# Moving a softmax ratio to GpSimd and reordering two other steps in a fused attention and gated-MLP kernel

## The chip, the cores and the metric

The kernel runs on one core of one Trainium2 chip. A core has five engines that run side by side, each in the order of its own instruction list: TensorE (PE in the profile; its weight loads are PEld), VectorE (DVE), ScalarE (ACT), GpSimd (POOL) and SyncE (SP, which only issues transfers here). They wait for each other through semaphores. The metric is the time of one execution on the device, in microseconds (us), as the median of several runs.

## The reference, cut to what matters

Two token mixers share one input `x` (2048 tokens of 512 values), and a gate per token blends them.

```
g   = sigmoid(sum(x * gate_w))
# mixer A: 32 heads of 16 values
q, k, v = x @ wqkv ;  pq = q @ w_phi ;  pk = k @ w_phi          (per head)
phi(p)  = concat(softmax(p), softmax(-p))                       (32 features per head)
kv  = phi(pk)^T @ v ;  z = sum over tokens of phi(pk)
a   = (phi(pq) @ kv) / (phi(pq) @ z + 1e-6) @ wo
# mixer B
z1, z2 = halves of gelu(x @ w_in) ;  z2 = layernorm(z2)
b   = (z1 * (w_sp @ z2 + b_sp)) @ w_out                          (w_sp: 2048 x 2048)
out = g * a + (1 - g) * b
```

## The kernel before

**Stages.** From 0 to about 44 us it computes `z1` and `z2` (`z_mm`, line 208). From 44 to about 124 us a loop over 16 tiles of 128 tokens makes the features of the keys (`k_tile`), the values (`v_tile`) and their product `kvacc` (`kv_acc`), four of the 16 query tiles (`q_tile`), and, interleaved, steps of the spatial product `w_sp @ z2`. From there to the end the remaining query tiles, the attention tiles (`attn_tile`), the rest of the spatial product and the output projections (`ba_tile`) run.

**The spatial product.** The rows of `w_sp` are taken as eight pairs p of row tiles (p and p+8). Pairs 0 and 5 are multiplied plainly (`plain`). The other six go by a scheme of seven products of half size instead of eight (`product(p, k)`, k = 1 to 7). It needs scaled sums of the weight blocks. For each pair ACT takes magnitudes of both halves (`w_size`, line 342, which the diff calls a magnitude pass: |w| summed per row; it also fills a scratch tile). DVE adds the two row sums (`wsum`, 347), PE sums over the rows (`w_level`, 351), and DVE makes the scale `wdown` and its inverse `wup` (352, 355). ACT scales one half by `wup` (`w_scale`, 370, about 2 us). Then `w_sum` forms the sums: S3 on DVE (358, output `wmix`), S1 on GpSimd (375), S2 on DVE (377), S4 on DVE (358, output `wsp`). A pair takes three steps of the token loop: (5, 2), (6, the next pair's 1, 7), (4, 3).

**Banks.** The products add up in three PSUM banks. One of them is opened by product 5 (`start=True`), read by DVE after product 7 and again after product 3 (`plus`, line 570, output `c`). So product 3 waits for the first read, and the next pair's product 5 for the second. `v_tile` has one bank: the values of tile t+1 can only be written when DVE has read those of tile t (`vr`, line 487). Attention tiles share one bank too, read by DVE at lines 613 and 614 (`o`).

**Features.** `expo` multiplies, takes exp(p) and exp(-p) on ACT (443) and sums each over the 16 features of a head on DVE (`zs`, 447). DVE takes reciprocals (`rk`, 456; `rq`, 473). `even_out` then forms a ratio of the two sums per head (462, 128 x 32 numbers, on DVE) and GpSimd multiplies the second half of the features by it (463). So both halves share one normaliser. For keys that normaliser goes into the values: `vr` is v times `rk`, and GpSimd copies `rk` itself beside it (486). The tile `zs` has two buffers, shared by keys and queries.

**What sets the order.** The lists of PE and ACT are in the order of the program text (`manual_schedule`). Those of DVE, GpSimd and SP come from a scheduler that takes ready instructions by priority. In the token loop, `prepare(tt, w_size)` stands ahead of the value tile, or, in every third tile, behind the first product of the step.

Of the kernel before, what the change touches and what calls it, by code (L numbers as in the profile page):

```python
# [8 lines left out]
ALU = mybir.AluOpType  # L9
# [5 lines left out]
P = 128  # L15
# [3 lines left out]
DH = 16  # L19
# [9 lines left out]
NG = 4  # L29
# [12 lines left out]
def kernel(  # L42
# [14 lines left out]
    nc = tc.nc  # L57
# [58 lines left out]
        out=ramp[:, 0, :], data0=ones32[:, :], data1=zeros[:, :], initial=0.0,  # L116
# [4 lines left out]
    for q in range(4):  # L121
        qs = slice(32 * q, 32 * q + 32)
        nc.vector.tensor_tensor(
            out=ident[qs, qs], in0=ramp[qs, 0, :], in1=ramp[qs, 1, :], op=ALU.is_equal)
    nc.gpsimd.memset(brow[:], 0.0)
    nc.gpsimd.memset(wphi[:], 0.0)
    def load_z2w(eng, dt):
# [11 lines left out]
        out=scrap[:, :], in_=nc.const_aps.tensor(1.0, [P, 1], BF16), func=AF.Gelu_apprx_tanh)  # L139
# [6 lines left out]
    for h in range(2):  # L146
        nc.sync.dma_start(
            out=w_z1[:, 2 * h:2 * h + 2, :], in_=w_in_v[:, 2 * h:2 * h + 2, 0:FH])
    for i in range(4, 8):
        x_dma_T(i)  # L150
    for q in range(2, NCH):
        nc.sync.dma_start_transpose(
            out=xT[:, :, q * CH:(q + 1) * CH], in_=x2[q * CH:(q + 1) * CH, :]
# [3 lines left out]
    for qk in (1, 0):  # L157
        nc.sync.dma_start_transpose(
            out=wqkT[:, qk * NDT:(qk + 1) * NDT, :], in_=A_wqkv[:, qk * D:(qk + 1) * D])
# [13 lines left out]
    for p in range(NRING):  # L173
# [4 lines left out]
        out=mask4[:], in_=mask4[:], pattern=[[-32, NG]],  # L178
# [3 lines left out]
        out=mask4[:], in_=mask4[:], pattern=[[32, NG]],  # L182
# [3 lines left out]
        out=mask64[:, :, :], in_=mask4[:, :, None].to_broadcast([P, NG, DH]))  # L186
# [204 lines left out]
    def z_sum(part, i):  # L391
        c = slice(4 * part, 4 * part + 4)
        out, a, op, b = Z_SUMS[i]
        nc.vector.tensor_tensor(
            out=zsums[out][:, c, :], in0=zsums[a][:, c, :], in1=zsums[b][:, c, :], op=op)
# [35 lines left out]
    def bank_tile(tag):  # L431
        return psM.tile([P, CH], FP32, name="mm", tag=tag)
# [20 lines left out]
    def k_tile(tt, bank):  # L453
        ek, z = expo(kvp, "ek", 5, tt, wk_p, bank_tile(bank))
        rk = kvp.tile([P, H, 2], FP32, name="rk", bufs=3)
        nc.vector.reciprocal(out=rk[:], in_=z[:])  # L456
        even_out(ek, z, rk[:, :, 1])
        return ek, rk

    def even_out(e, z, rz):  # L460
        ratio = work.tile([P, H], FP32, name="ratio")
        nc.vector.tensor_tensor(out=ratio[:], in0=z[:, :, 0], in1=rz, op=ALU.mult)  # L462
        nc.gpsimd.tensor_tensor(  # L463
            out=e[:, :, 1, :], in0=e[:, :, 1, :],
            in1=ratio[:, :, None].to_broadcast([P, H, DH]), op=ALU.mult)
# [4 lines left out]
    def q_tile(n, ps):  # L470
        eq, z = expo(work, "eq", 3, token(n), wq_p, ps)
        rq = work.tile([P, H], FP32, name="rq")
        nc.vector.reciprocal(out=rq[:], in_=z[:, :, 1])
        even_out(eq, z, rq[:])
        eqT = work.tile([P, 8, P], BF16, name="eqT", bufs=7)
        nc.sync.dma_start_transpose(out=eqT[:, :, :], in_=eq[:].rearrange("p h a f -> p (h a f)"))
        eqTs[n] = eqT

    def v_tile(tt, rk, bank):
        v_ps = bank_tile(bank)  # L480
        for dt in range(NDT):
            nc.tensor.matmul(v_ps[:, :], lhsT=xT[:, dt, tt * P:(tt + 1) * P], rhs=wv_sb[:, dt, :],  # L482
                             start=(dt == 0), stop=(dt == NDT - 1))
        vr = kvp.tile([P, 8, AW], BF16, name="vr", bufs=4)
        r0 = rk[:, :, 0].rearrange("p (u h) -> p u h", u=8)
        nc.gpsimd.tensor_copy(out=vr[:, :, 64:AW], in_=r0)
        nc.vector.tensor_tensor(  # L487
            out=vr[:, :, 0:64].rearrange("p u (h d) -> p u h d", d=DH),
            in0=v_ps[:, :].rearrange("p (u h d) -> p u h d", u=8, d=DH),
            in1=r0[:, :, :, None].to_broadcast([P, 8, NG, DH]),  # L490
            op=ALU.mult,
        )
        return vr

    def kv_acc(tt, ek, vr):
        ekf = ek[:].rearrange("p h a f -> p (h a f)")
        for g in range(8):
            nc.tensor.matmul(
                kvacc[:, g, 0:AW], lhsT=ekf[:, g * P:(g + 1) * P], rhs=vr[:, g, :],
                start=(tt == 0 and g % 4 == 0), stop=(tt == NT - 1), skip_group_check=True,  # L500
            )

    def kvz_evac():
        nc.vector.tensor_tensor(
            out=kvz[:, :, 0:64], in0=kvacc[:, :, 0:64],
            in1=mask64[:].rearrange("p h d -> p (h d)")[:, None, :].to_broadcast([P, 8, 64]),
            op=ALU.mult,
        )
        nc.vector.scalar_tensor_tensor(
            out=kvz[:, :, 64:AW], in0=kvacc[:, :, 64:AW],  # L510
            scalar=0.5e-6, in1=mask4[:, None, :].to_broadcast([P, 8, NG]),
            op0=ALU.add, op1=ALU.mult,
        )
# [157 lines left out]
    steps, work_at = [], {}  # L671
# [28 lines left out]
    def prepare(n, *kinds):  # L700
        for f, *args in work_at.get(n, ()):
            if f in kinds:
                f(*args)

    def level(n):
        for f, p, *_ in work_at.get(n, ()):
            if f is w_scale:
                w_level(p, bank_tile(Q_BANK if n < NT else X_TAGS[2]))
# [3 lines left out]
    with tc.manual_schedule(engines={mybir.EngineType.PE, mybir.EngineType.Activation}):  # L712
        ks = {0: k_tile(0, Q_BANK)}
        kvacc = psM.tile([P, 8, P], FP32, name="kvacc", tag="kvat", bufs=1)
        pend = []
        for tt in range(NT):
            if tt + 1 < NT:
                ks[tt + 1] = k_tile(tt + 1, K_BANK)
            prepare(tt, w_load, load_w_out)
            if tt % 3 != 2:  # L720
                prepare(tt, w_size)
            if tt < 4:
                z_sum(1, tt)
            ek, rk = ks.pop(tt)
            pend.append((tt, ek, v_tile(tt, rk, V_BANK if tt != 1 else X_TAGS[2])))
            level(tt)
            prepare(tt, w_sum)
            if len(pend) == 3:
                kv_acc(*pend.pop(0))
            for i, part in enumerate(steps.pop(0)):  # L730
                part[0](*part[1:])
                if i == 0:
                    prepare(tt, w_scale, *[w_size] * (tt % 3 == 2))
            if tt in Q_AT:
                q_tile(Q_AT.index(tt), bank_tile(Q_BANK))
        nc.scalar.activation(out=g_el[:, :], in_=glog[:, :], func=AF.Exp)
        nc.vector.tensor_scalar(out=g_1p[:, :], in0=g_el[:, :], scalar1=1.0, scalar2=None, op0=ALU.add)
        nc.vector.reciprocal(out=g_inv[:, :], in_=g_1p[:, :])
        for p_ in pend:
            kv_acc(*p_)  # L740
        kvz_evac()
# [86 lines left out]
```

## Time and profile before

| | |
|---|---|
| median of 3 runs | 204.14 us (204.03 to 204.48) |
| profiled execution | 203.92 us, of which 202.2 us span from first to last instruction |
| PE busy | 195.5 us (97%) |
| DVE, ACT, GpSimd busy | 152.2, 126.4, 85.7 us |
| granted TensorE clock | 1.0 throughout |

The profile's rows give, in this order: engine, line of the program, operation, output and inputs by the program's names, and shapes. In the listing by time the first two numbers are start and duration in us, and a bracket gives the engine's idle time before the row and what ended it. Rows of several instructions are merged ("x8"). Matmuls of PE overlap each other, so the start of the next row says more than a duration. The end of a wait is inferred from semaphores and can name the wrong one of several. Now and then a matmul record is missing (a row "x3" of four).

Busy times by stretch show the middle stage's period: between the scalings (line 370) of pairs 2, 3 and 4, at 72.27, 88.18 and 104.10 us, lie 15.91 and 15.92 us, in which DVE is busy 13.97 and 13.99 us, GpSimd 11.44 and 11.46, ACT 12.62 and 12.57.

### The profile page before, as it was taken

Reading aid. Unit: us, or ns where it says so; the run is one execution under the profiler, and the core shown is the slowest. Engines: PE = TensorE matmul, PEld = TensorE weight load, DVE = VectorE, ACT = ScalarE, POOL = GpSimd, SP = SyncE. Lnnn points to the kernel's source line nnn. Section 1 sums busy time; section 2 is a strip of 40 time slices with the busy share of each in tenths; the row PEclk is TensorE's granted clock in tenths of the full one; section 3 lists DMA queues with packets and bytes.
Section 4 is the critical chain, followed back from the end, with each engine's and each line's share of the span. In section 5 each row is a group of like instructions: output and inputs, shape, how many; then the busy total and the mean of one; then the engine's idle time right before and its main releaser. Section 6 shows DMA issues by size and latency. Waiting matters only on the chain.

```text
span 202.2 us, 3982 instructions
## 1 busy us (share of the span) xinstructions
PE 195.5 (97%) x1474; PEld 116.7 (58%) x1491; DVE 152.2 (75%) x308; ACT 126.4 (63%) x183; POOL 85.7 (42%) x102
## 2 busy tenths in 40 slices
PE   8999999999999999999899999989999999999994
PEld 4666666665565665565465666655555555555542
DVE  4469676969979869969969995997797676675400
ACT  3466677789759489669857377775655356343222
POOL 6020202020547529658677677363345233433400
PEclk9999999999999999999999999999999999999999
DMA  5999396998034704921941926954968988896261
GB/s 197 238 178 127 67 232 134 186 209 215 2 42 93 153 3 62 224 57 29 220 88 24 187 52 167 194 111 81 165 132 168 123 184 170 166 165 137 54 153 52
DMA packets 89210, 26.50 MB, mean 131 GB/s; under 512 B 84536, under 2 KB 89064, under 8 KB 89192
## 3 DMA queue, kind: packets, MB, share of 16 engines
q1 hardware_dynamic: 86448, 23.32, 61.6%
q10 hardware_dynamic: 2600, 2.42, 4.3%
q0 software_dynamic: 144, 0.52, 0.9%
q8 instruction: 11, 0.18, 0.4%
q14 instruction: 7, 0.06, 0.1%
HBM read 3.45 MB, written 2.10 MB: 27 GB/s over the span
## 4 chain that ended last, share of the span: by engine, by line
PE 57%; DVE 27%; ACT 7%; issue 4%; DMA 2%; POOL 1%; SPq 1%; DVEq 0%; ACTq 0%
PE zp L208 15%; PE mm L563 12%; PE mm L633 10%; DVE zs L447 8%; PE mm L628 7%; PE mm L439 6%; ACT wsp L370 4%; DVE wmix L358 4%; DVE vr L487 3%; DVE rk L456 2%; DVE ratio L462 2%; PE at L604 2%; ACT wmix L342 2%; DMA eqT<-eq 2%; PE zp L239 1%
## 5 line engine op out<-in xcount | busy, mean ns | idle before, releaser
L208 PE MATMUL zp<-w_z,xT 128*128 128x344 bf16 (+1 forms) x254 | 38.5, 311 | 0.4 <-DVE glog L224 0.4
L208 PEld LDWEIGHTS <-xT 128*128 128x128 bf16 x254 | 24.6, 98 | 12.5 <-issue 0.3
L463 POOL TENSOR_TENSOR eq<-eq,ratio 128x512 bf16<-128x512 bf16 x16 | 18.2, 1136 | 28.2 <-ACT ob L645 11.5
L563 PEld LDWEIGHTS <-wsp 128*128 128x128 f16 (+1 forms) x240 | 22.9, 98 | 12.3 <-issue 0.4
L577 POOL TENSOR_TENSOR z1all<-c,z1all 128x344 bf16<-128x344 f32 x24 | 23.0, 970 | 6.6 <-DVE c L570 4.3
L443 ACT ACTIVATE eq<-mm 128x512 bf16<-128x512 f32 x32 | 17.3, 594 | 12.6 <-PE mm L439 9.0
L563 PE MATMUL mm<-z2all,wsp 128*128 128x344 f16 x144 | 23.9, 309 | 0.0
L645 ACT ACTIVATE ob<-mm,g_inv 128x512 bf16<-128x512 f32 (+1 forms) x16 | 10.9, 681 | 20.0 <-PE mm L633 17.3
L633 PE MATMUL mm<-w_out_sb,uT 128*128 128x512 bf16 (+2 forms) x102 | 23.3, 366 | 0.0
L342 ACT ACTIVATE wmix<-wsp 128x2048 bf16<-128x2048 bf16 x12 | 23.0, 1919 | 0.0
L447 DVE TENSOR_REDUCE zs<-eq 128x64 f32<-128x1024 bf16 x16 | 19.4, 1210 | 4.6 <-ACT eq L443 4.6
L463 POOL TENSOR_TENSOR ek<-ek,ratio 128x512 bf16<-128x512 bf16 x16 | 20.1, 1259 | 1.6 <-DVE ratio L462 1.1
L531 PE MATMUL mm<-z2all,wsp 128*128 128x344 f16 x128 | 20.0, 309 | 0.0
L447 DVE TENSOR_REDUCE zs<-ek 128x64 f32<-128x1024 bf16 x16 | 19.2, 1207 | 0.2 <-ACT ek L443 0.2
L443 ACT ACTIVATE ek<-mm 128x512 bf16<-128x512 f32 x32 | 17.3, 599 | 2.2 <-PE mm L439 2.2
L375 POOL TENSOR_TENSOR wsp<-wsp 128x1024 f16<-128x1024 f16 x6 | 12.7, 2123 | 13.7 <-DVE wmix L358 13.7
L439 PEld LDWEIGHTS <-xT 128*128 128x128 bf16 x128 | 11.7, 97 | 10.1
L482 PE MATMUL mm<-wv_sb,xT 128*128 128x512 bf16 x64 | 16.4, 379 | 1.0 <-DVE vr L487 0.9
L223 ACT ACTIVATE z2raw<-zp 128x688 bf16<-128x688 f32 x16 | 11.8, 744 | 7.9 <-PE zp L208 7.8
L628 PE MATMUL mm<-wo_t,oT 128*128 128x512 bf16 (+2 forms) x65 | 16.3, 366 | 0.2
L633 PEld LDWEIGHTS <-uT 128*128 128x128 bf16 x102 | 9.8, 98 | 11.2
L439 PE MATMUL mm<-wk_p,xT 128*128 128x512 bf16 x57 | 15.9, 379 | 0.4
(100 smaller groups left out, 312.4 us busy)
## 6 DMA issues: line engine op xcount, KB each, us to landing
out_dram<-ob ACTq DMA_DIRECT2D x14, 128.0 KB, 2.0
w_z<-in_B_w_in_dram SPq DMA_DIRECT2D x2, 344.0 KB, 4.1
w_out_sb<-in_B_w_out_dram SPq DMA_DIRECT2D x1, 640.0 KB, 4.5
wv_sb<-in_A_wqkv_dram SPq DMA_DIRECT2D x1, 512.0 KB
wo_t<-in_A_wo_dram POOLq DMA_DIRECT2D x1, 512.0 KB, 5.1
w_z<-in_B_w_in_dram ACTq DMA_DIRECT2D x2, 172.0 KB, 3.3
w_z<-in_B_w_in_dram SPq DMA_DIRECT2D x2, 172.0 KB, 3.2
wsp<-in_B_w_sp_dram SPq DMA_TRANSPOSE x16, 5.3
```

The costliest lines, as they stand in the source:

```text
L208: nc.tensor.matmul(zp[:, j, 0:n], lhsT=xT[:, dt, tt * P:(tt + 1) * P], rhs=wt[:, dt, j * HF:j * HF + n], start=(dt == 0), stop=(dt == NDT ...
L342: nc.scalar.activation(out=wmix[p].bitcast(BF16).rearrange("p k s c -> p (k s c)"), in_=wraw[p][:, h * NT:(h + 1) * NT, :].rearrange("p s ...
L439: nc.tensor.matmul(ps[:, :], lhsT=xT[:, dt, tt * P:(tt + 1) * P], rhs=w[:, dt, :], start=(dt == 0), stop=(dt == NDT - 1))
L443: nc.scalar.activation(out=e[:, :, a, :], in_=ps[:, :].rearrange("p (h f) -> p h f", f=DH), func=AF.Exp, scale=1.0 - 2.0 * a)
L447: nc.vector.tensor_reduce(out=z[:].rearrange("p h a -> p (h a)"), in_=e[:].rearrange("p h a f -> p (h a) f"), axis=AX.X, op=ALU.add,)
L463: nc.gpsimd.tensor_tensor(out=e[:, :, 1, :], in0=e[:, :, 1, :], in1=ratio[:, :, None].to_broadcast([P, H, DH]), op=ALU.mult)
L482: nc.tensor.matmul(v_ps[:, :], lhsT=xT[:, dt, tt * P:(tt + 1) * P], rhs=wv_sb[:, dt, :], start=(dt == 0), stop=(dt == NDT - 1))
L531: nc.tensor.matmul(x, lhsT=wraw[t % HS][:, h * NT + st, :], rhs=z2all[:, st, j * HF:(j + 1) * HF], start=(st == 0), stop=(st == NT - 1))
L563: nc.tensor.matmul(x, lhsT=w_part(p, wa)[:, st, :], rhs=zsums[zb][:, st, :], start=(k in OPENS and st == 0), stop=(st == HS - 1), skip_gro ...
L577: nc.gpsimd.tensor_tensor(out=zu, in0=o, in1=zu, op=ALU.mult)
L628: nc.tensor.matmul(acc, lhsT=oTs[n][:, g, :], rhs=wo_t[:, g, c0:c1], start=start and g == 0, stop=stop and g == NG - 1)
L633: nc.tensor.matmul(acc, lhsT=uTs[n][:, ft, :], rhs=w_out_sb[:, ft, c0:c1], start=start and ft == 0, stop=stop and ft == NFT - 1)
```

## The change

There are three edits.

1. The ratio of line 462 is computed by GpSimd instead of DVE, for keys and queries (16 + 16 instructions).
2. The product `vr` (line 487, after the change 488) is issued at high priority, so that the scheduler puts it ahead of other ready work on DVE.
3. Which tiles of the token loop take the magnitude pass behind the first product is now told by that product (k = 1 or 6) instead of by every third tile.

```
     def even_out(e, z, rz):
         ratio = work.tile([P, H], FP32, name="ratio")
-        nc.vector.tensor_tensor(out=ratio[:], in0=z[:, :, 0], in1=rz, op=ALU.mult)
+        nc.gpsimd.tensor_tensor(out=ratio[:], in0=z[:, :, 0], in1=rz, op=ALU.mult)
         nc.gpsimd.tensor_tensor(
             out=e[:, :, 1, :], in0=e[:, :, 1, :],
...
-        nc.vector.tensor_tensor(
-            out=vr[:, :, 0:64].rearrange("p u (h d) -> p u h d", d=DH),
-            in0=v_ps[:, :].rearrange("p (u h d) -> p u h d", u=8, d=DH),
-            in1=r0[:, :, :, None].to_broadcast([P, 8, NG, DH]),
-            op=ALU.mult,
-        )
+        with tc.high_priority():
+            nc.vector.tensor_tensor(
+                out=vr[:, :, 0:64].rearrange("p u (h d) -> p u h d", d=DH),
+                in0=v_ps[:, :].rearrange("p (u h d) -> p u h d", u=8, d=DH),
+                in1=r0[:, :, :, None].to_broadcast([P, 8, NG, DH]),
+                op=ALU.mult,
+            )
...
             prepare(tt, w_load, load_w_out)
-            if tt % 3 != 2:
+            late = steps[0][0][0] is product and steps[0][0][2] in (1, 6)
+            if not late:
                 prepare(tt, w_size)
...
                 if i == 0:
-                    prepare(tt, w_scale, *[w_size] * (tt % 3 == 2))
+                    prepare(tt, w_scale, *[w_size] * late)
```

## The prediction

> **What bounds the kernel now.** I read the busy shares first, then the chain that ended last, then the token loop in order of time.
>
> ```profile
> PE 195.5 (97%) x1474; PEld 116.7 (58%) x1491; DVE 152.2 (75%) x308; ACT 126.4 (63%) x183; POOL 85.7 (42%) x102
> PE 57%; DVE 27%; ACT 7%; issue 4%; DMA 2%; POOL 1%; SPq 1%; DVEq 0%; ACTq 0%
> ```
>
> PE looks full, yet over a quarter of the chain is DVE. One period of the token loop by time (start, duration, row) shows why:
>
> ```profile
> 84.24 1.02 PE L482 MATMUL mm<-wv_sb,xT 128*128 128x512 bf16 x4 [0.39 <-DVE vr L487]
> ...
> 88.18 2.00 ACT L370 ACTIVATE wsp<-wsp,wup 128x2048 f16<-128x2048 bf16 x1 [0.79 <-DMA eqT<-eq]
> 90.21 1.28 DVE L358 SCALAR_TENSOR_TENSOR wmix<-wsp,wup 128x1024 f16<-128x1024 bf16 x1 [1.85 <-ACT wsp L370]
> ...
> 93.67 2.08 POOL L577 TENSOR_TENSOR z1all<-c,z1all 128x344 bf16<-128x344 f32 x2
> ...
> 94.58 1.08 ACT L443 ACTIVATE eq<-mm 128x512 bf16<-128x512 f32 x2
> ...
> 94.97 0.82 DVE L462 TENSOR_TENSOR ratio<-zs,rk 128x32 f32<-128x32 f32 x1
> ...
> 95.72 0.56 DVE L570 SCALAR_TENSOR_TENSOR c<-mm,wdown,u 128x344 f32<-128x344 f32 x1
> ...
> 96.21 1.20 DVE L447 TENSOR_REDUCE zs<-eq 128x64 f32<-128x1024 bf16 x1
> ...
> 96.34 2.14 PEld L563 LDWEIGHTS <-wsp 128*128 128x128 f16 x15 [0.23 <-issue]
> ...
> 99.42 0.69 DVE L487 TENSOR_TENSOR vr<-mm,rk 128x512 bf16<-128x512 f32 x1
> 99.54 1.05 POOL L463 TENSOR_TENSOR eq<-eq,ratio 128x512 bf16<-128x512 bf16 x1
> ...
> 100.02 1.65 DVE L358 SCALAR_TENSOR_TENSOR wsp<-wsp,wup,wmix 128x1024 f16<-128x1024 bf16 x1
> 100.16 1.02 PE L482 MATMUL mm<-wv_sb,xT 128*128 128x512 bf16 x4 [0.47 <-DVE vr L487]
> ...
> 104.10 2.00 ACT L370 ACTIVATE wsp<-wsp,wup 128x2048 f16<-128x2048 bf16 x1 [0.80 <-DVE wup L355]
> ```
>
> Three things are to be seen. First, a closed loop: scaling (370), `wmix`, `c`, then DVE without a pause to the next `wup`, next scaling: 104.10 − 88.18 = 15.92 us per pair. (The transfer named at 88.18 was not the cause: `wup` ended at 88.09.) PE needs less: 7 products of 1.17, 7 tile multiplications of 0.86 and 3 `kvacc` of 0.26 are 15.0. Second, the difference appears as PE waiting: the value tile starts 0.56 late at 84.24 and 0.63 at 100.16 (pace: 0.86 after the key tile) because `vr` stands behind two sums and two ratios; product 5 starts 0.29 late at 96.34 because `c` stands behind a ratio. Third, that ratio costs 0.82 where others cost 0.19: it ends at 95.79, just after GpSimd's `z1all` rows do (95.75). The same holds at 51.59, 79.06, 110.89 and 115.69, each ending with a GpSimd row.
>
> All late starts of PE after 44 us: 0.17 (55.1), 0.26 (63.2), 0.56, 0.29, 0.63, 0.27 (112.25) and 0.80 (133.79, an attention tile waiting for `o`): 2.98 us. That is the most this change can give, as PE's list is the same in the changed program.
>
> **Part 1: the ratio leaves DVE.** Gone from DVE are 16 key ratios of 388 ns and 16 query ratios of 170 ns on average, 8.9 us. After 135 us PE starts nothing late, so those there are worth nothing. Per loop: between scaling and query sum the blocked ratio holds DVE for 0.75 (94.97 to 95.72), but the sum also needs the query's exponentials, which ACT, busy throughout from 88.18, delivers at 95.66. So 8.03 (88.18 to 96.21) becomes about 7.5, not 7.28: 0.5 gained. Between query sum and next scaling (7.89) two short ratios free about 0.2. The S4 row (1.65 at 100.02) runs in 1.27 when alone; now it is held by `eq` on GpSimd until 100.59. With `eq` earlier this shrinks by 0 to 0.35; I take 0.1. The loop is then 7.5 + 7.6 = 15.1, with bounds 14.9 and 15.3; PE's 15.0 is the floor. Two loops give 2 × 0.8 = 1.6 (1.2 to 1.8).
>
> **What GpSimd pays.** No row shows a two-input 128x32 product in float32 there. The nearest groups (count, busy us, mean ns, idle before), and from the waits GpSimd's before S1 (total, times, longest):
>
> ```profile
> L486 POOL CAST vr<-rk 128x32 bf16<-128x32 f32 x16 | 3.4, 211 | 21.3 <-DVE rk L456 8.3 <-DVE wsum L347 6.4 <-DVE wup L355 4.7
> L290 POOL TENSOR_TENSOR rstd<-veps,mhalf 128x4 f32<-128x4 f32 x4 | 4.2, 1042 | 0.3
> ```
>
> ```profile
> POOL wsp L375 <- DVE wmix L358: 13.7, 6, 4.5
> ```
>
> From below: 0.21, the one-input copy of the same shape. From above: 1.04, the only two-input float32 row, but that is a power. The multiplications (1.06 for 512 columns, 0.84 for 344) scale to under 0.1 plus a fixed part near the copy's; I take 0.3, near the copy. Four per loop add 1.2 to GpSimd's 11.45; it waits about 2 us per loop for `wmix` ahead of S1, which takes that up. Key features are used two tiles later, query features after 124 us. For the last key tile `ek` ended at 122.87, ahead of its product at 123.4; `wo_t`'s transfer issue (0.99) stands between copy and `ek` as before, and ratio and copy end about when DVE's ratio did. The ratio waits at the head of GpSimd's queue for `rk`, with copy, `ek`, `z1all` and S1 behind it; before, the copy waited there for the same `rk`.
>
> The Trainium skill (GPSIMD Engine Reference, Engine selection) speaks against the move: elementwise work on two inputs belongs on VectorE, being about twice as slow on GpSimd. Twice the unblocked 0.19 would be 0.38, or 0.3 us more per loop on GpSimd and, while its wait lasts, nothing on the total. Its page SBUF — State Buffer (Who interferes with whom) says that a VectorE instruction with two SBUF inputs and a GpSimd instruction that reads SBUF exclude each other, the later blocking fully. The 0.82 rows agree; by that rule the block would now fall on the GpSimd side or on S4, which is the 0.1 against 0.35 above.
>
> **A new wait.** `zs` has two buffers, and its reader is now on GpSimd: the sum of tile n+2 must wait for the ratio of tile n. The tightest is the key sum after the query sum, at about 9.6 us after a scaling (7.5, query sum 1.12, `vr` 0.60, `rq` 0.33); the ratio it needs stands behind S1 and two `z1all` rows, which end at 95.75, or 7.6; with 0.3 it is done at 7.9. Margin 1.7 us: no cost. Behind that sum stand `rk`, S4, `vr` and `wup`, so a wait there would lengthen the loop one for one.
>
> **Part 2: `vr` ahead.** In the changed order it stands ahead of the next key sum. Its values are ready about 0.3 us sooner than the key's exponentials (tile multiplication end against two ACT rows of 0.55), so DVE does not idle for it. The value tiles no longer wait: the late starts 0.26, 0.56 and 0.63 go. Only the first is a gain of its own (the others are the loop's); with 0.17 at 55.1, where the row sum `wsum` moves ahead, PE has 0.43 more at the start. `wup` of pair 2 comes only about 0.3 sooner; I take 0.3 (0 to 0.43).
>
> **Part 3: magnitude passes.** ACT's list differs in one place: near 64 us the bank seed (550) runs ahead of one pass (1.9). The seed needs product 1, so the pass ends about 1.5 us later (66.2 to 67.7). `wsum` then comes at 67.8, where S4 behind it waits for PE until 68.02 anyway (about 67.6 if PE is 0.43 ahead). Cost 0.2 at most, inside the 0 to 0.43 above. SP's list is unchanged, so no transfer moves past another.
>
> **After the loops.** Product 5 at 112.25 no longer waits for the ratio at 110.89: 0.25 (0 to 0.27). At 133.79 `o` waits behind `wmix` (2.09, held by `eq` until 131.90). `eq` starts some 0.2 sooner: 0.2. It could also be later by a dear GpSimd ratio and cost 0.3, or the whole 0.8 could go.
>
> **Sum.** 0.3 + 1.6 + 0.25 + 0.2 = 2.35; the new coupling between DVE and GpSimd I charge with 0.1 per loop, 2.15 in all. The profiled execution took 203.92 (span 202.2), which is 0.22 below the median; 201.8 against it is 202.0 against the median. The bounds of the terms give gains from 0.9 (0 + 1.2 + 0 − 0.3) to PE's 2.98: 203.2 to 201.2.
>
> **Rivals.**
> - PE becomes the only bound: all 2.98 go, 201.2. For: PE's floor of 15.0 lies 0.1 under my loop. Against: ACT's 7.5 and the wait at 133.8.
> - The block only changes its victim: GpSimd's extra rows hold S4, S2 or `wmix` on DVE as long as the ratio was held, 0.6 per loop. Then 1.6 shrinks to 0.4, sum about 0.95: 203.2.
> - Nothing: `vr` and ratio only trade places, the loop stays at 15.9, the gain is the head's alone: 203.9.
> - Slower: GpSimd becomes the loop. This begins where a ratio costs 0.3 + (2 − 1.2)/4 = 0.5 us, when the wait ahead of S1 is used up, and the key sum then waits at its buffer. At the upper row's 1.04 it is 4 × 0.54 = 2.2 us per loop over its slack, on top of 15.0: 17.2 against 15.92, for two loops 2.6 slower, less 0.5 gained elsewhere: 206.2; a price half-way gives about 204.9. For: the one float32 row. Against: the copy of the same shape, strides and engine.
>
> **How the numbers follow.** About 0.2% (0.4 us) is what a measurement of this kernel can tell from no change. Forecast 0.52 (its own range 201.4 to 202.8), PE bound 0.10, changed victim 0.18, nothing 0.07, slower 0.13. Faster 0.80, same 0.07, slower 0.13. The range 201.2 to 204.2 leaves out the slower case and a little below.
>
> **What would show it.** Right: scalings of pairs 2, 3 and 4 about 15.1 apart; no row of PE 482 waiting for `vr`; ratio rows on GpSimd near 0.3. Wrong: those rows above 0.5, sums (447) waiting for GpSimd's ratio, S4 or `wmix` rows of DVE near 2 us in each loop, or a new PE wait for `c` at product 3.

## The result, and the profile after

| | kernel before | changed kernel |
|---|---|---|
| median | 204.03 us (15 runs) | 202.33 us (15 runs, 201.74 to 204.57) |
| ratio, 95% interval | | 0.9932 (0.9903 to 0.996) |
| a second time | 204.08 us (23 runs) | 202.47 us (6 runs): 0.9912 (0.9885 to 0.9938) |

The change makes the kernel 1.6 to 1.7 us faster. The forecast was 2.1 us.

The profiled execution of the changed kernel took 204.44 us (span 202.6), among its longest. Its extra time lies behind all the work that the change touches: its last matmul ends at 197.69, and a second profile (202.45 us, span 200.6) has it at 197.75. The 2 us lie behind the issue of the last transfer (198.11 and 198.16). So, beside the medians, I compare what lies between two points that every profile has: the first key tile of the token loop and the last matmul.

The page of the profile after, busy shares and chain:

```profile
PE 194.9 (96%) x1474; PEld 116.7 (58%) x1491; DVE 143.8 (71%) x276; ACT 126.5 (62%) x183; POOL 92.8 (46%) x134
PE 80%; DVE 8%; ACT 4%; issue 2%; DMA 2%; POOL 1%; SPq 0%; DVEq 0%; ACTq 0%
```

DVE's share of the chain has fallen from 27% to 8%, PE's risen from 57% to 80%. The same period of the token loop by time in the profile after (start, duration, row):

```profile
87.44 2.00 ACT L370 ACTIVATE wsp<-wsp,wup 128x2048 f16<-128x2048 bf16 x1 [0.61 <-DVE wup L355]
89.47 1.28 DVE L358 SCALAR_TENSOR_TENSOR wmix<-wsp,wup 128x1024 f16<-128x1024 bf16 x1 [2.12 <-ACT wsp L370]
...
93.83 1.08 ACT L443 ACTIVATE eq<-mm 128x512 bf16<-128x512 f32 x2
...
94.36 1.03 PE L482 MATMUL mm<-wv_sb,xT 128*128 128x512 bf16 x4
...
95.02 0.26 POOL L462 TENSOR_TENSOR ratio<-zs,rk 128x32 f32<-128x32 f32 x1
...
95.38 1.22 DVE L447 TENSOR_REDUCE zs<-eq 128x64 f32<-128x1024 bf16 x1 [0.96 <-POOL ratio L462]
...
98.67 1.03 PE L482 MATMUL mm<-wv_sb,xT 128*128 128x512 bf16 x4
...
99.32 1.18 DVE L358 SCALAR_TENSOR_TENSOR wsp<-wsp,wup,wmix 128x1024 f16<-128x1024 bf16 x1
99.48 1.15 POOL L462 TENSOR_TENSOR ratio<-zs,rk 128x32 f32<-128x32 f32 x1 [0.56 <-DVE rk L456]
...
102.94 2.00 ACT L370 ACTIVATE wsp<-wsp,wup 128x2048 f16<-128x2048 bf16 x1 [1.11 <-DVE wup L355]
```

Four things are to be seen. The scalings are now 15.17 (72.27 to 87.44) and 15.50 apart. No value tile (482) waits for `vr`: key tile and value tile follow at 0.86 (93.50 and 94.36). The ratio costs GpSimd 0.26, except where it runs beside one of DVE's sums: here S4 takes 1.18 (1.65 before), and GpSimd's ratio is held for 1.15. And the query sum at 95.38 has DVE idle for 0.96, though ACT's query exponentials ended at 94.91.

### The profile page after: what moved, and what is told of

Its sections match the earlier page's. It is cut to its first block, busy times and chain, and to the rows that moved or that the text cites. A ratio compares the mean times of both kernels' runs of the same rounds, so it can differ in the third digit from the quotient of the medians.

```text
span 202.6 us, 3982 instructions
## 1 busy us (share of the span) xinstructions
PE 194.9 (96%) x1474; PEld 116.7 (58%) x1491; DVE 143.8 (71%) x276; ACT 126.5 (62%) x183; POOL 92.8 (46%) x134
## 4 chain that ended last, share of the span: by engine, by line
PE 80%; DVE 8%; ACT 4%; issue 2%; DMA 2%; POOL 1%; SPq 0%; DVEq 0%; ACTq 0%
PE mm L564 21%; PE zp L208 15%; PE mm L439 12%; PE mm L634 10%; PE mm L629 7%; PE mm L532 6%; PE mm L482 6%; PE at L605 2%; DVE zs L447 2%; DMA w_z<-in_B_w_in_dram 2%; ACT wmix L342 2%; PE kvacc L499 1%; DVE zmix L394 1%; ACT wsp L370 1%; DVE bn L226 1%
## 5 line engine op out<-in xcount | busy, mean ns | idle before, releaser
L375 POOL TENSOR_TENSOR wsp<-wsp 128x1024 f16<-128x1024 f16 x6 | 12.7, 2122 | 13.9 <-DVE wmix L358 13.9
L443 ACT ACTIVATE ek<-mm 128x512 bf16<-128x512 f32 x32 | 17.2, 599 | 2.4 <-PE mm L439 2.4
L463 POOL TENSOR_TENSOR eq<-eq,ratio 128x512 bf16<-128x512 bf16 x16 | 16.9, 1056 | 1.3
L463 POOL TENSOR_TENSOR ek<-ek,ratio 128x512 bf16<-128x512 bf16 x16 | 16.8, 1053 | 0.0
L287 POOL TENSOR_SCALAR veps<-mv 128x4 f32<-128x4 f32 x4 | 0.9, 228 | 34.4 <-DVE mv L227 34.4
L462 POOL TENSOR_TENSOR ratio<-zs,rq 128x32 f32<-128x32 f32 x16 | 5.5, 341 | 24.0 <-DVE rq L473 14.5
```

Source lines behind the costliest of these rows:

```text
L443: nc.scalar.activation(out=e[:, :, a, :], in_=ps[:, :].rearrange("p (h f) -> p h f", f=DH), func=AF.Exp, scale=1.0 - 2.0 * a)
L463: nc.gpsimd.tensor_tensor(out=e[:, :, 1, :], in0=e[:, :, 1, :], in1=ratio[:, :, None].to_broadcast([P, H, DH]), op=ALU.mult)
```

## The experiments

Every profile was cut at the same PE rows: first key tile of the token loop (line 439; 44.27 in the kernel before), the 6th, 9th and 12th product `kvacc` (498), which are two pair loops apart by one each, and the end of the last matmul. Differences of these starts, in us:

| kernel | to 6th kvacc | loop 1 | loop 2 | rest | sum | median, ratio to before (95%) |
|---|---|---|---|---|---|---|
| before | 35.96 | 15.56 | 15.92 | 87.69 | 155.13 | |
| changed (1+2+3) | 35.53 | 15.00 | 15.33 | 87.14 | 153.00 | 202.33, 0.9932 (0.9903 to 0.996) |
| changed, again | 35.53 | 15.00 | 15.33 | 87.14 | 153.00 | 202.47, 0.9912 (0.9885 to 0.9938) |
| part 1 alone | 35.77 | 15.00 | 15.03 | 87.14 | 152.94 | 202.05, 0.9872 (0.9827 to 0.9917) |
| part 2 alone | 35.77 | 15.35 | 15.66 | 88.66 | 155.45 | 204.13, 0.9992 (0.997 to 1.0014) |
| part 3 alone | 35.96 | 15.58 | 15.92 | 87.69 | 155.15 | 204.26, 1.0004 (0.9978 to 1.003) |
| parts 1+3 | 35.56 | 15.00 | 15.05 | 87.14 | 152.75 | 202.31, 0.9905 (0.9879 to 0.9932) |
| parts 1+2 | 35.77 | 15.00 | 15.33 | 87.14 | 153.24 | 202.25, 0.9903 (0.9881 to 0.9925) |
| changed, 4 buffers of zs | 35.53 | 15.00 | 15.21 | 87.08 | 152.81 | 201.65, 0.987 (0.9822 to 0.9918) |
| 1+3, 4 buffers of zs | 35.63 | 15.00 | 15.04 | 87.08 | 152.75 | 201.61, 0.9889 (0.9862 to 0.9917) |
| key ratios only | 35.77 | 15.37 | 16.05 | 87.44 | 154.64 | 203.77, 0.9977 (0.9947 to 1.0007) |
| spare ratio on DVE | 36.07 | 15.44 | 15.46 | 87.94 | 154.91 | 204.42, 1.0022 (0.9993 to 1.0052) |
| ratio twice | 36.32 | 15.35 | 15.85 | 87.61 | 155.12 | 204.05, 0.9993 (0.9965 to 1.0021) |
| ratio four times | 35.53 | 15.00 | 16.80 | 96.10 | 163.42 | 212.36, 1.0418 (1.0372 to 1.0463) |

The two profiles of the changed kernel agree in every column to 0.01. So tenths can be read here, which the medians can't give: their intervals are some 0.5% wide. The other kernels have one profile each.

### Each part alone

Part 1:

```
-        nc.vector.tensor_tensor(out=ratio[:], in0=z[:, :, 0], in1=rz, op=ALU.mult)
+        nc.gpsimd.tensor_tensor(out=ratio[:], in0=z[:, :, 0], in1=rz, op=ALU.mult)
```

> The kernel before with part 1 alone: the 32 ratios on GpSimd; vr stays behind the next key sum, the magnitude passes stay where they were. Theory A (the ratio's time on VectorE set the loop of two pairs, as the prediction's sum has it: 1.6 for the loops and 0.45 behind them, less 0.2): a gain of 1.3 to 1.9 us, scalings (370) of pairs 2, 3 and 4 about 15.2 to 15.4 apart, and value tiles (482) that still wait up to 0.3 for vr. Theory B (the order of vr did it, the ratio only changed engines): a gain under 0.5 us and loops of 15.8 to 15.9. Theory C (each part alone only moves the wait; both are needed): gains of e1 and e2 that add up to less than 1.2 us.

Theories B and C are out, and A fits best, but the gain lies above its 1.3 to 1.9: 2.19 us in the trace (155.13 to 152.94), a ratio of 0.9872. That is all of the changed kernel's gain (2.13). PE hardly waits in the loops (15.00 and 15.03; I had PE's floor at 15.0), and no value tile waits more than 0.04, though `vr` still stands behind the key sum.

Part 2:

```
-        nc.vector.tensor_tensor(
-            out=vr[:, :, 0:64]...
+        with tc.high_priority():
+            nc.vector.tensor_tensor(
+                out=vr[:, :, 0:64]...
```

> The kernel before with part 2 alone: vr ahead of the next key sum, the ratios on VectorE. Theory A: 0.3 us from the start of the token loop (late starts 0.17 and 0.26 at 55.1 and 63.2) and nothing in the loops, because vr and the sum only trade places in an unbroken VectorE queue: 0.2 to 0.5 us, scalings still 15.8 to 15.9 apart, though no value tile waits for vr any more. Theory B: 1.2 to 1.7 us, scalings 15.2 to 15.5 apart.

No gain, where theory A had 0.2 to 0.5: ratio 0.9992, and 0.32 more in the trace. It does take 0.19 out of the start and 0.5 out of the two loops, but the attention stage gives 0.97 back. Its rows by time (part 2 alone):

```profile
99.22 1.83 DVE L358 SCALAR_TENSOR_TENSOR wsp<-wsp,wup,wmix 128x1024 f16<-128x1024 bf16 x1
...
103.60 2.00 ACT L370 ACTIVATE wsp<-wsp,wup 128x2048 f16<-128x2048 bf16 x1 [1.45 <-DVE wup L355]
...
106.18 1.33 PE L564 MATMUL mm<-zmix,wsp 128*128 128x344 f16 x8 [0.39 <-ACT u L546]
...
130.98 2.09 DVE L358 SCALAR_TENSOR_TENSOR wmix<-wsp,wup 128x1024 f16<-128x1024 bf16 x1
132.99 0.74 DVE L615 SCALAR_TENSOR_TENSOR o<-at,g_el,rden 128x512 bf16<-128x512 f32 x1
...
133.88 0.41 PE L605 MATMUL at<-kvz,eqT 128*128 128x68 bf16 x8 [1.45 <-DVE o L615]
```

The value tiles' wait is gone and has become one of product 4 for ACT, whose `u` stands behind the late scaling, and a longer one of the attention tile for `o`. DVE's queue is as long as before (152.2 us busy in both); it only serves another customer first. DVE starts that `o` 88.56 us after the first key tile, against 88.63 in the kernel before: PE arrives earlier and waits. Not all of the 0.97 is part 2's, though: 0.38 of it arises at an attention tile at 163.52 that waits for a transfer (`eqT`), and only one other profile (four ratios, below) has such a wait. So the 0.32 is not shown to be a loss; without that wait part 2 alone stands where the kernel before does.

Part 3:

```
-            if tt % 3 != 2:
+            late = steps[0][0][0] is product and steps[0][0][2] in (1, 6)
+            if not late:
                 prepare(tt, w_size)
...
-                    prepare(tt, w_scale, *[w_size] * (tt % 3 == 2))
+                    prepare(tt, w_scale, *[w_size] * late)
```

> The kernel before with part 3 alone: the bank seed ahead of one magnitude pass near 64 us. By the prediction a loss of 0 to 0.2 us, which a measurement of this kernel can hardly tell from no change; scalings as before (58.1, 72.3, 88.2, 104.1). Rival: the row sum that comes 1.5 us later stops S4 behind it, and the second scaling comes 0.3 or more later.

Nothing, as expected: 1.0004, 155.15 against 155.13. S4 starts 0.44 later after the first key tile than in the kernel before (24.19 against 23.75), but takes 1.27 in place of 1.58, and the second scaling comes at the same distance (28.00).

### Part 2 and part 3 on top of part 1

> Parts 1 and 3 without part 2: ratios on GpSimd, one magnitude pass behind the bank seed near 64 us, vr in its old place behind the next key sum. In the run of part 1 alone, product 3 of the first pair started 0.21 us late because the seed (550) ran behind that pass. If part 3 is worth something only once part 1 has brought VectorE forward, that late start is gone here, the time from the first key tile of the token loop to the last matmul is 152.7 us (152.94 with part 1 alone, 153.00 in the changed kernel), and the ratio to the kernel before is 0.985 to 0.990. If part 2 is needed for the loops, they are 15.3 or longer and the ratio is 0.992 or more.

> Parts 1 and 2 without part 3: the magnitude pass stays ahead of the seed. If part 3 removes what part 1 turns up, product 3 of the first pair waits here 0.2 to 0.5 us for the seed and the time is 0.2 to 0.5 us above the changed kernel; if part 3 does nothing, it is the changed kernel's (202.4).

Both expectations on part 3 hold in the trace (the ratio 0.9905 lies just above the range given for the first; the product in question is product 2, the third of its step; I misnamed it: it adds to the bank that the seed copies). By time, part 1 alone, ACT and PE:

```profile
63.49 1.91 ACT L342 ACTIVATE wmix<-wsp 128x2048 bf16<-128x2048 bf16 x1
64.57 1.33 PE L563 MATMUL mm<-zmix,wsp 128*128 128x344 f16 x8
65.29 0.20 ACT L342 ACTIVATION_READ_ACCUMULATOR wmix<-wsp 128x1 f32 x1
65.38 0.52 ACT L550 ACTIVATE mm<-mm,wup 128x344 f32<-128x344 f32 x1
65.95 1.33 PE L563 MATMUL mm<-z2all,wsp 128*128 128x344 f16 x8
```

The same with part 3 added:

```profile
64.55 1.33 PE L563 MATMUL mm<-zmix,wsp 128*128 128x344 f16 x8
64.75 0.52 ACT L550 ACTIVATE mm<-mm,wup 128x344 f32<-128x344 f32 x1 [1.17 <-PE mm L563]
65.20 1.90 ACT L342 ACTIVATE wmix<-wsp 128x2048 bf16<-128x2048 bf16 x1
65.72 1.33 PE L563 MATMUL mm<-z2all,wsp 128*128 128x344 f16 x8
```

In the first the seed (550) ends at 65.90 because the magnitude pass stands ahead, and PE's rows are 1.38 apart; in the second 1.17. So part 3 takes 0.21 (1+3) and 0.24 (1+2+3 against 1+2) off the start of the loop, once part 1 has brought PE forward. By itself it has nothing to remove, since PE then comes to that place later.

Part 2 on top of 1+3 costs: 153.00 against 152.75, all of it in loop 2 (15.33 against 15.05). On top of part 1 without part 3 it is 0.30 (153.24 against 152.94), again in loop 2. The medians don't separate these kernels; this rests on traces, of which the changed kernel's repeats to 0.01.

### The query sum that starts late

> The changed kernel unaltered, beside the others on one chip, with a second profile. In its first profile the query sum at 95.38 started 0.47 us after ScalarE's last query exponential, where the same sums at 79.89 and 110.21 started 0.11 and 0.10 after theirs, and the loop that followed took 15.50. If that belongs to the kernel (order of vr, buffers of zs), it is here again, and the time is 0.3 us or more above part 1 alone (ratio to the kernel before about 0.993 against 0.987). If it was one execution's, both loops are 15.0 to 15.2 and the ratio to the kernel before is 0.987 to 0.990.

It is the kernel's own: in the second profile the sum again starts late, 0.48 after ACT's last query exponential, and both loops repeat. It is there with parts 1+2, with the ratio computed twice and, without part 2, with key ratios only (0.46 to 0.48); not with part 1 alone or with 1+3 (0.10 each), nor, though part 2 is in, with the spare ratio or the ratio computed four times (0.11 each; these kernels come below).

```
-        z = work.tile([P, H, 2], FP32, name="zs")
+        z = work.tile([P, H, 2], FP32, name="zs", bufs=4)
```

> The changed kernel with four buffers for the sums zs in place of two. In the profile after, the query sum at 95.38 starts 0.47 us after ScalarE's last query exponential and is put down to GpSimd's ratio. In the program it waits for that exponential and for the ratio two sums back, which ended near 87.7. If the buffer is what holds it (theory Z), this kernel's loops are both 15.1 to 15.2 and it is 0.3 to 0.4 us faster than the changed kernel. If the wait was long satisfied, as the prediction's margin of 1.7 us has it, the loops stay at 15.2 and 15.5 and the time is that of the changed kernel (202.3).

With four buffers, where the program has no wait for GpSimd in front of the query sums any more, they start 0.03 after the exponentials, and loop 2 of the changed kernel shrinks from 15.33 to 15.21, the sum by 0.19. That is less than theory Z asked for, and the medians are not comparable this closely. Nor is the late sum all that part 2 costs: with four buffers loop 2 is 15.21 with it and 15.04 without it (1+3, four buffers). So of the 0.28 some 0.12 goes with the late sum, and the rest is not traced to a row. What holds the sum is not settled: by the program's semaphore values it waits for the ratio two sums back, which ended at 87.68, nearly 8 us earlier. The ratio that the profile names can't be the one it waits for: with part 1 alone the same sum starts at 94.33, while that ratio runs until 94.55. Yet in four of the five late cases the sum starts 0.10 to 0.11 behind that ratio's end. The buffers take part in it, and I have no run that tells more.

> Parts 1 and 3 with four buffers for zs: the candidate for the fastest. If the query sums' start behind the exponentials (0.10 with two buffers, 0.03 with four, in the traces) is worth anything, 0 to 0.1 us below parts 1 and 3 with two buffers; since the token loop then has PE as its bound (15.0 a loop), I expect no difference between these two: 0.985 to 0.990.

As expected: 152.75 with two buffers and with four. This one had the lowest median (201.61), but against the changed kernel's 0.9912 (0.9885 to 0.9938) its 0.9889 (0.9862 to 0.9917) is no proven gain.

### Is it DVE's time, and which of it?

```
+        spare = work.tile([P, H], FP32, name="spare")
+        nc.vector.tensor_tensor(out=spare[:], in0=z[:, :, 0], in1=rz, op=ALU.mult)
         nc.gpsimd.tensor_tensor(out=ratio[:], in0=z[:, :, 0], in1=rz, op=ALU.mult)
```

> The changed kernel with every ratio computed a second time on VectorE, into a tile that nobody reads, where VectorE computed it before; the ratio that is used stays on GpSimd. VectorE's load is that of the kernel before again. If the gain is VectorE's freed time (the prediction's view), it goes: within 0.6 us of the kernel before, loops of 15.5 to 15.9, spare rows of about 0.8 where GpSimd's z1all rows run. If the gain comes from ek and eq being ready earlier because GpSimd no longer waits for VectorE's ratio, it stays: 201.8 to 202.6.

The gain goes: 1.0022. The rows of the spare ratio, by its tile (count, least, median and longest duration in ns):

```profile
L463 DVE TENSOR_TENSOR spare<-zs,rk x16: 191/250/2470, 52.4 to 120.6; 128x32 f32<-128x32 f32 x16
L463 DVE TENSOR_TENSOR spare<-zs,rq x16: 122/192/559, 83.7 to 180.7; 128x32 f32<-128x32 f32 x16
```

So it is mainly DVE's queue that pays, not the moment at which GpSimd gets its ratio. In the trace 0.22 is left of the gain: loops of 15.44 and 15.46, but a start and a rest that are 0.36 longer than before. The two loops keep 0.58 of their 1.15, but they are then close to those of part 2 alone (30.90 against 31.01 for both), where GpSimd still waits for DVE's ratio. So little of the loops' gain is left for GpSimd's own ratio.

```
     def even_out(e, z, rz, keys):
         ratio = work.tile([P, H], FP32, name="ratio")
-        nc.vector.tensor_tensor(out=ratio[:], in0=z[:, :, 0], in1=rz, op=ALU.mult)
+        eng = nc.gpsimd if keys else nc.vector
+        eng.tensor_tensor(out=ratio[:], in0=z[:, :, 0], in1=rz, op=ALU.mult)
```

> The kernel before with only the 16 key ratios on GpSimd; the query ratios (0.12 to 0.17 us where nothing blocks them) stay on VectorE. The blocked row of each loop (0.82) is a key ratio, and so are two of the three short ones. If VectorE's time ahead of the scaling is what counts, nearly all of part 1's gain is here: 1.8 to 2.2 us, loops of 15.0 to 15.3. If all four ratios of a loop matter alike, half of it: about 1.1 us, loops near 15.5.

A plain miss. With the dear ratios gone from DVE, and only rows of 0.13 to 0.19 left, most of the gain should be there; 0.3 us is (0.9977), and loop 2 is longer than before. By time, key ratios only, DVE and GpSimd:

```profile
97.34 1.21 DVE L447 TENSOR_REDUCE zs<-ek 128x64 f32<-128x1024 bf16 x1
...
98.47 0.34 DVE L474 RECIPROCAL rq<-zs 128x32 f32<-128x32 f32 x1
...
99.14 0.13 DVE L463 TENSOR_TENSOR ratio<-zs,rq 128x32 f32<-128x32 f32 x1
...
99.74 1.06 POOL L464 TENSOR_TENSOR eq<-eq,ratio 128x512 bf16<-128x512 bf16 x1
99.85 2.03 DVE L358 SCALAR_TENSOR_TENSOR wsp<-wsp,wup,wmix 128x1024 f16<-128x1024 bf16 x1
100.76 2.04 POOL L464 TENSOR_TENSOR ek<-ek,ratio 128x512 bf16<-128x512 bf16 x1
```

The query ratio takes 0.13, but DVE reaches it only at 99.14. So `eq` runs at 99.74, just ahead of S4, and S4 takes 2.03; with part 1 alone `eq` ran at 97.35, right behind `rq` and ratio, and S4 took 1.61. What matters of a row is also when the row that it releases on the other engine runs, and whom that one holds up. This is read from the rows; no run moves `eq` alone.

### What a dearer ratio on GpSimd does

```
         nc.gpsimd.tensor_tensor(out=ratio[:], in0=z[:, :, 0], in1=rz, op=ALU.mult)
+        nc.gpsimd.tensor_tensor(out=ratio[:], in0=z[:, :, 0], in1=rz, op=ALU.mult)
```

> The changed kernel with each ratio computed twice on GpSimd: about 0.27 + 0.35 = 0.62 us in place of 0.27, 1.4 us more per loop. The prediction put the turning point at 0.5 us a ratio, so GpSimd's backlog should begin here: a query sum or two waiting for GpSimd's ratio, loops of 15.0 to 15.7, and the last key tile's ek (0.6 us ahead of its product in the changed kernel) late by 0 to 2 us: 202.4 to 205. If the slack is larger, the time is the changed kernel's.

The whole gain is gone at twice (0.9993), as the prediction's turning point of 0.5 us has it, but not by its mechanism. GpSimd is not full. Its wait ahead of S1, from the waits of the ratio computed twice (total, times, longest):

```profile
POOL wsp L375 <- DVE wmix L358: 11.9, 5, 5.3
```

against 13.9 in the changed kernel; in each loop it still waits 1.65 there, against 2.0. The largest piece is in the start (36.32 against 35.53), and it goes at S4, by time in the same kernel:

```profile
67.35 1.06 POOL L464 TENSOR_TENSOR ek<-ek,ratio 128x512 bf16<-128x512 bf16 x1
67.45 0.97 DVE L347 TENSOR_TENSOR wsum<-wsum 128x1 bf16<-128x1 f32 x1 [0.90 <-ACT wmix L342]
...
68.34 1.94 DVE L358 SCALAR_TENSOR_TENSOR wsp<-wsp,wup,wmix 128x1024 f16<-128x1024 bf16 x1
68.36 0.84 POOL L579 TENSOR_TENSOR z1all<-c,z1all 128x344 bf16<-128x344 f32 x1
```

In the changed kernel these two DVE rows take 0.35 and 1.27. Counted from the first key tile, `ek` comes 0.61 later and `z1all` 0.41, and they now lie on these rows: 1.3 us of DVE ahead of a scaling, behind which PE waits 0.52 for ACT's `u` (75.29). This is my rival "the block only changes its victim", called up by half a microsecond of delay. The further 1.3 us in the loops and the rest I have not followed row by row; S4 takes 1.68 and 1.98 in two of the three later pairs, against 1.18 and 1.29.

Four times:

> The changed kernel with each ratio computed four times over on GpSimd, into the same tile: a price of 4 x 0.26 = 1.04 us (plus what repeated issues cost) in place of 0.26, 3.1 us more of GpSimd per loop. By the prediction GpSimd's idle time ahead of S1 (about 2 us per loop) is used up at 0.5 us a ratio, and at 1.04 the loop is GpSimd's: 17.2 us, the whole about 206.2. If GpSimd's slack is larger than I counted, the loops stay under 16 and the time under 204.

The second loop between scalings was 17.06 (86.65 to 103.71; 17.2 expected), the whole 6 us longer than expected. The waits of that kernel:

```profile
PE kvacc L502 <- POOL ek L466: 4.3, 1, 4.3
DVE zs L447 <- POOL ratio L465: 3.8, 3, 1.7
```

The backlog does not end with the loops: the last key tile's `ek` comes 4.3 us after PE is ready for it, and the rest takes 96.10 instead of 87.14. I had ended the sum at the loops. (A repeated ratio also comes every 0.35, not 0.26.)

The wait has a second price, on PE itself. The 16 matmuls behind it:

```profile
128.40 4.78 PE L535 MATMUL mm<-z2all,wsp 128*128 128x344 f16 x16
```

In the kernel before they take 2.49. The granted clock, 1.0 ahead of the wait, is 0.50 from 128 to 132 us here and 1.0 again from 134.6. From the last but one `kvacc` to the second attention tile this makes 13.70 us, against 6.32 in the changed kernel: 4.5 of waiting and 2.9 of slower matmuls.

The start and the first loop of this kernel, on the other hand, are those of the changed one (35.53, 15.00), with S4 at 1.28 and 1.22. So a dearer ratio does not cost in proportion to its price: twice costs there by where its rows fall, four times does not.

## Why the prediction was right, and where not

**The ceiling and the sum.** All late starts of PE were 2.98 us; 0.88 of them are left (0.22 and 0.12 at products 4 and 3 of loop 2, 0.54 at the attention tile). The trace gives 155.13 − 153.00 = 2.13, against 2.15 predicted. The medians moved by 1.70 and 1.61. Both profiled executions of the changed kernel entered the token loop 0.42 to 0.48 later (44.69, 44.75) than the one of before (44.27), which would account for the difference. Nearly all of it is there at 7 us, far ahead of the first row that the change moves: the second one-column matmul of line 247 starts at 6.80 before, and at 7.22 and 7.18 in these two. The starts of the token loop vary between 43.74 and 44.75 over the 14 profiles without following the parts; whether the medians carry such a difference is open.

**The terms.**

| term | predicted | trace |
|---|---|---|
| start, by part 2 | 0.3 (0 to 0.43) | 0.43, of which part 1 alone has 0.19 and parts 1+3 have 0.40 |
| two loops | 1.6, less 0.2 for coupling | 1.15 |
| product 5, attention tile | 0.25 + 0.2 | 0.55 |
| ratio on GpSimd | 0.3 | 0.25 to 0.27 alone, 1.15 to 1.25 beside S4 |

The loops are the term that was too large: the first came out at 15.00 on PE, the second kept 0.34 of late starts. A step that failed is "A new wait ... no cost". I looked at the key sum behind the query sum and found 1.7 us of margin; it was the query sum that started late, 0.47 after its input, and with it the scaling at 102.94. Its size is some 0.12, by the run with four buffers; the rest of loop 2's late starts goes with part 2. The start was too small, the errors cancelled, and the sum looks better than its parts.

**Part 2** is the step that failed in kind. I gave it the start's gain ("the late starts 0.26, 0.56 and 0.63 go"), and they do go with it. But they go with part 1 too, since a shorter DVE queue reaches `vr` earlier in any order. By itself part 2 is no gain, and on top of 1+3 it costs 0.25 in the trace. I had no rival in which one part of the change works against another.

**Part 3** was costed at up to 0.2 of loss. It is a gain of 0.21 to 0.24 behind part 1. I asked what the moved pass delays, not what it had been delaying: the seed, behind which PE would wait as soon as it was 0.4 us earlier.

**The block.** That the block would fall on GpSimd or on S4 was right. S4 went from 1.65 to 1.18, by more than the 0.1 I took, and GpSimd's ratio took the 1.15, where it cost nothing. The loops did not need it: with part 1 alone S4 stays at 1.61, and they are PE's. The rule in the Trainium skill (SBUF — State Buffer, Who interferes with whom) fits these rows. The other rule weighed, that elementwise work on two inputs is about twice as slow on GpSimd (GPSIMD Engine Reference, Engine selection), is milder here: 0.26 against 0.19 on DVE, 1.4 times.

**The rivals.** "PE only" is true of the loops in part 1 alone and of no whole kernel. "Changed victim" did not happen at 0.26 and did at twice that. "GpSimd becomes the loop" had the right turning point by luck: at twice the price GpSimd still waited 1.65 us ahead of S1 in each loop. Its price at four times was short by the 4.3 us at the last key tile and the slower matmuls that follow.

## What to carry to other kernels

List PE's late starts and ask of each what would remove it; where two edits remove the same ones, credit them once, and the dearer edit may turn into a loss. A row moved to another engine is worth not its duration but what the rows behind it then collide with: here 0.35 us more per ratio on GpSimd undid 2 us. And a reordering that costs nothing today should be asked what it will free once the others are in, since a stall that goes uncovers the next one.

## What I had not expected of the hardware

The start of the kernel differs between profiles by more than parts 2 and 3 are worth. First `z` matmul, by time, in the kernel before:

```profile
4.31 0.49 PE L208 MATMUL zp<-w_z,xT 128*128 128x344 bf16 x1
```

and in the profile of part 1 alone:

```profile
4.46 0.31 PE L208 MATMUL zp<-w_z,xT 128*128 128x344 bf16 x1
```

The granted clock is 1.0 in both at that time, the matmuls the same up to there. In the first, matmuls of 344 columns come 0.28 apart until 5.75 us, in the second 0.14. That is about the pace (0.29) at which they come behind the 4.3 us wait of the kernel with four ratios, where the granted clock does read 0.50. Together with early waits this puts the token loop's start anywhere from 43.74 to 44.75 us: the seven profiles in which the second one-column matmul of line 247 starts by 6.53 us enter the loop by 44.00, the other seven (6.80 and later) from 44.27 on. So whole times mix it in, and a few tenths between two kernels are only to be had from pieces of the trace.
